# The second token group's plain feature blocks: 8 instead of 10, with block scales built by GpSimd, reordered steps, and one pair of query loads split over two queues

## The chip, the cores and the metric

The kernel runs on one core of a Trainium2 chip. The metric is the device time of one execution in microseconds (us); several executions are made and the median is quoted. One further execution is recorded by the hardware profiler. Engines are named as in the profile: PE is TensorE (PEld its weight loads), DVE is VectorE, ACT is ScalarE, POOL is GpSimd, SP is SyncE, which here only issues transfers; POOL issues transfers too, and "SPq" and "POOLq" are their queues.

## The reference

A retention layer (a linear recurrence with one decay per head) feeds a feed-forward layer whose activation is h * erf(softplus(h)).

```python
# q, k, v: (4, 8, 768, 64) float32
gamma = 1.0 - 2.0 ** (-5.0 - np.arange(H))
for t in range(S):
    state = gamma * state + einsum('bhd,bhe->bhde', k[:, :, t], v[:, :, t])
    y[:, :, t] = (1 / sqrt(D)) * einsum('bhd,bhde->bhe', q[:, :, t], state)
x = y.transpose(0, 2, 1, 3).reshape(B * S, H * D)      # (3072, 512)
h = x @ w_in                                           # w_in (512, 2048), float64
g = h * erf(log1p(exp(h)))
out = g @ w_out                                        # w_out (2048, 512), float64
```

## The kernel before

**Tiling.** The 3072 tokens are 24 chunks of 128 (six per batch), and two chunks make a group of 256: groups 0 to 11. The 2048 hidden features are 16 blocks of 128 (`ft`); a piece of `w_in` holds two blocks (pieces 0 to 7). The order of all work on every engine is written out by hand in the source; each engine runs its own list in that order and waits at an instruction whose inputs or buffer are not ready, with everything behind it on that engine.

**Two ways to make the hidden values.** Plain: `hidden_of` multiplies float32 operands, 256 columns at a time (L698), and needs only the converted weight piece `WF`. Split: weights and x are each cut into hi, lo and dif parts of a faster type, and each product is three matmuls. `unit(g, n)` does that for one group and one piece (two blocks, 256 columns, L732); `pair_unit(g, ft)` does it for one block and two neighbouring groups at once (512 columns, L766). `ALONE` says which blocks a group has by itself: group 0 all 16 plain, group 1 its first 10 plain, the last group half by `unit`. Blocks 10 to 15 of groups 1 and 2 are joined, blocks 8 and 9 of group 2 are done by `unit(2, 4)`, and blocks 0 to 7 of group 2 are joined with group 3 in the period after.

**The first 24 us** do the retention of chunks 0 to 3 (groups 0 and 1) in the simple form (`ret_out`, `ret_add`: copies of x L539, L540, states L547). **The plain loop**, `for ft in range(n_ft)`, then runs over the 16 blocks. Each turn has its matmuls, `need(...)`, which advances the conversion of float64 weights to float32 on DVE (per piece: exponents L235, then L249, L254, L258, L270, with an ACT step L238 between) until the piece wanted next is there, the extra work that the table `during` lists for that `ft`, and `put_hidden`: an ACT copy out of PSUM (L712 for two groups, L709 for one) and a POOL transfer to scratch (L714, L710). The h tiles come from a pool of six (`small`, tag b2). In this loop chunks 4 and 5 (group 2) go through the retention: transposes, `begin` at ft 6, `states` at 7, `results` at 8, `crossed_sums` at 9. Also in the loop: x of groups 1 and 2 is split (`split_x`, L332 on ACT, L333 and L334 on DVE), pieces 4 and 5 are split (`split_weights`: L312 on ACT, L325 and L326 on DVE), and the first block pair of chunks, 6 and 7, is loaded and prepared.

**Pairs of chunks.** `load_pair(j)` loads k and v in rows by POOL (four transfers of 256 KB) and k and q once more in 32-row blocks (`KB`, `QB`) by SP: 16 + 16 transfers of 32 KB (L164), each of 128-byte runs. `prepare(j)` is one DVE transpose of `KB` (L565), a multiplication of `QB` by the table `kq_b` (L560), and a transpose of `QB`. `steps(pair, n)` advances the loads. `load_block_scales` fetches the first column of that table and its factors by 20 small POOL transfers (L407, L413), and `block_scales` finishes it: three DVE instructions (L419 to L421) and five POOL multiplications (L423).

**Periods.** After the loop, period 2 runs `unit(2, 4)` and six joined units, and each later period eight units, with `begin` and `results` of the next pair between them (`joined(at, to, g)`: before unit 3 and unit 5), split weights, the next pair's loads, and each unit's put: for joined units of group 1 two ACT copies and a 512 KB POOL transfer of a high and a low part (L777 to L779, tile in the 34-buffer pool b4), later an ACT and a DVE instruction (L340, L341) into a b2 tile. PSUM banks o0 to o3 alternate between units, so a unit's put must be through before the second unit after it starts. At the end the projection with `w_out` (L981) reads the hidden values back; where they were stored as high and low parts, `add_lows` adds them on DVE (L917).

Of the kernel before, what the change touches and what calls it, by code (L numbers as in the profile page):

```python
# [13 lines left out]
F32 = mybir.dt.float32  # L14
F32R = mybir.dt.float32r
U32 = mybir.dt.uint32
I64 = mybir.dt.int64
AF = mybir.ActivationFunctionType
ALU = mybir.AluOpType
# [13 lines left out]
def head(u, r):  # L33
    return u // 2 + u % 2 * 4 + 2 * r
# [15 lines left out]
def kernel(  # L50
# [23 lines left out]
    DH = d_model // 2  # L74
    FIRST = JPC // 2 - 1

    ALONE = {0: n_ft, 1: 5 * n_ft // 8, NG - 1: n_ft // 2}
    assert D == 64 and d_model == H * D and n_k == HP == 4 and S % GT == 0 and NJ % 2 == 0
    assert H == 8 and n_ft == 16 and NC > JPC and GT == 2 * C

# [69 lines left out]
    def load_pair(j):  # L150

        b, c = divmod(j, NC)
        KNP[j] = b4("kn", [2, H, D])
        KB[j], QB[j] = (b4(name, [HP, 2 * C]) for name in ("kb", "qb"))
        for i in range(2):
            load_values(j + i, nc.gpsimd)
            KN[j + i], SLOT[j + i] = KNP[j][:, i], head
            nc.gpsimd.dma_start(KN[j + i], of_chunk(k, j + i))
        yield
        for to, src in ((KB[j], k), (QB[j], q)):  # L160
            for s, d in itertools.product(range(2), range(2)):
                part = slice((2 * s + d) * 32, (2 * s + d + 1) * 32)
                for u in range(HP):
                    nc.sync.dma_start(  # L164
                        to[part, u].rearrange("p (a d) -> p a d", d=32),
                        src[b, head(u, s), c * C : (c + 2) * C, d * 32 : (d + 1) * 32].rearrange(
                            "(a p) d -> p a d", p=32
                        ),
                    )
                yield  # L170

    kq_s = const.tile([P, NC, 2, H], F32, name="kq_s")
# [226 lines left out]
        query_scale(slice(2, NC))  # L399


    kq_b = const.tile([P, 2, HP, NC, 4], F32, name="kq_b")
    by_b = const.tile([P, 2, HP], F32, name="by_b")

    def load_block_scales():
        for s, i in itertools.product(range(2), range(2)):
            nc.gpsimd.dma_start(  # L407
                by_b[s * D : (s + 1) * D, 1, 2 * i : 2 * i + 2], decay_s[i * D : (i + 1) * D, s::2]
            )
        for s, d in itertools.product(range(2), range(2)):  # L410
            part = slice((2 * s + d) * 32, (2 * s + d + 1) * 32)
            for u in range(HP):
                nc.gpsimd.dma_start(  # L413
                    kq_b[part, 0, u, 0],
                    decay_k[:, head(u, s) : head(u, s) + 1].rearrange("(a p) h -> p (a h)", p=32),
                )

    def block_scales():
        nc.vector.reciprocal(by_b[:, 0], by_b[:, 1])  # L419
        nc.vector.reciprocal(kq_b[:, 1, :, 0], kq_b[:, 0, :, 0])  # L420
        nc.vector.tensor_scalar(kq_b[:, 1, :, 0], kq_b[:, 1, :, 0], unscale, None, op0=ALU.mult)  # L421
        for c in range(1, NC):
            nc.gpsimd.tensor_tensor(  # L423
                kq_b[:, :, :, c], kq_b[:, :, :, c - 1],
                by_b[:, :, :, None].to_broadcast([P, 2, HP, 4]), op=ALU.mult,
            )

    psum_turn = itertools.cycle((ps_r, ps_h))
# [124 lines left out]
    def prepare(j):  # L553


        for name, store, x in (("k", KT, KB[j]), ("q", QT, QB[j])):
            if name == "q":
                own = x.rearrange("p u (a d) -> p u a d", d=32)
                scale = kq_b[:, 1, :, j % NC : j % NC + 2].rearrange("p u c a -> p u (c a)")
                nc.vector.tensor_tensor(  # L560
                    own, own, scale[:, :, :, None].to_broadcast([P, HP, 8, 32]), op=ALU.mult
                )
                yield
            t = b4(name + "T", [HP, 2 * C])
            nc.vector.transpose(t.rearrange("p u t -> p (u t)"), x.rearrange("p u t -> p (u t)"))  # L565
            for i in range(2):
                store[j + i] = t[:, :, i * C : (i + 1) * C]
            yield

        if j > 2 * JPC:  # L570
            yield from values(j)
# [93 lines left out]
    def crossed_sums(j):  # L665
        g, i = divmod(j, 2)
        for r in range(2):
# [4 lines left out]
            else:  # L672
                nc.vector.tensor_tensor(x, x, SC[j][a][:, 2:, :D], op=ALU.add)

    def split_x(j, n=1):
        g, i = divmod(j, 2)
        if i == 0:
            if not XR:
                XR.extend(
                    ring.tile([P, 3, HP, GT], F32R, name=f"x_{x}", tag=f"x{i}")  # L680
                    for i, x in enumerate(("hi", "lo", "dif"))
                )
            X[g] = [x[:, g % 3] for x in XR]
        at = slice(i * C, (i + n) * C)
        split(X[g], (slice(None), slice(None), at), XC[g][:, :, at])

# [151 lines left out]
    ret_out(JPC - 1, lambda: hidden_of(0, 0), state_last=True)  # L838
    need("in", 1)
    hidden_of(1, 0)  # L840
    A(JPC - 1)


    def steps(s, n=1):
# [11 lines left out]
        5: [(scale_early, b, 0), (T, b, None, ("o0", "o1")), (steps, pair, 2)],  # L856
        6: [(begin, a, ps_r), (begin, b, None, ("o2", "o3")), (steps, pair)],
        7: [(states, a), (states, b)],
        8: [(results, a, ("o0", "o1")), (results, b), (block_scales,)],
        9: [(crossed_sums, a), (crossed_sums, b), (convert, 2), (split_x, a, 2)],  # L860
        10: [(hi_of, 4), (steps, vals, 1)],
        12: [(split_weights, 4), (hi_of, 5)],
        13: [(split_x, 2, 2), (steps, vals, 1)],
        14: [(split_weights, 5)],
        15: [(steps, prep, 3)],
    }
# [149 lines left out]
    def period(g, prep, next_prep):  # L1016

        a, b = 2 * g + 2, 2 * g + 3
        one, two = partial(partial, unit), partial(partial, pair_unit)
        if g == G2:  # L1020
            units = [one(g, 4)] + [two(1, ft) for ft in range(ALONE[1], n_ft)]
            return units, joined(3, 5, g), {
                0: [(hi_of, 6)],
                1: [(split_weights, 6)],
                2: [(hi_of, 7)],
                3: [(states, a), (states, b), (split_weights, 7)],
                4: [(hi_of, 0), (split_weights, 0)],
                5: [(crossed_sums, a), (crossed_sums, b), (split_x, a, 2)],
                6: [(hi_of, 1), (split_weights, 1), (steps, next_prep, 1)],
            }, range(4)  # L1030
        if g < NG:
            units = [two(g - 1, ft) for ft in range(8 - 8 * (g % 2), 16 - 8 * (g % 2))]
        if g == G2 + 1:
            return units, joined(3, 5, g), {
                0: [(steps, vals), (hi_of, 2), (steps, prep, 1)],
                1: [(steps, prep, 1), (steps, vals)],
                2: [(split_weights, 2), (hi_of, 3)],
                3: [(states, a), (states, b), (split_weights, 3)],
                5: [(crossed_sums, a), (crossed_sums, b), (split_x, a, 2)],
                7: [(steps, next_prep, 1)],  # L1040
            }, range(4)
        if g < NG - 2:
            return units, joined(2, 5, g), {
                0: [(steps, prep, 4)],
                1: [(convert, 2)],
                2: [(states, a), (convert, 1)],
                3: [(states, b), (convert, 1)],
                4: [(convert, 2 if g < 8 else 1)],
                5: [(crossed_sums, a), (crossed_sums, b)],
                6: [(split_x, a, 2)],  # L1050
                7: [(steps, next_prep, 1 if g < NG - 3 else 4), (convert, 1)],
            }, LOADS.get(g, ())
        if g == NG - 2:
            return units, joined(1, 3, g), {
                0: [(steps, prep, 4), (load_w_out, 0)],
                1: [(states, a), (load_w_out, 1)],
                2: [(states, b), (split_w_out, 0)],
                3: [(crossed_sums, a), (crossed_sums, b)],
                4: [(split_w_out, 1), (load_hiddens, 0)],
                5: [(split_x, a, 2)],  # L1060
                6: [(softplus, 0), (load_w_out, 2)],
                7: [(erf, 0), (gated, 0)],
            }, ()
        if g == NG - 1:
            return units, {}, {
                0: [(split_g, 0), (split_w_out, 2), (load_w_out, 3)],
                1: [(split_g, 1), (load_hiddens, 1)],
                2: [(split_w_out, 3)],
                3: [(softplus, 1), (load_w_out, 4)],
                4: [(erf, 1)],  # L1070
                5: [(split_w_out, 4), (load_w_out, 5)],
                6: [(gated, 1)],
                7: [(split_g, 2), (load_hiddens, 2)],
            }, ()
        return [one(NG - 1, n) for n in range(NPC // 2, NPC)], {}, {
            0: [(split_w_out, 5), (load_w_out, 6)],
            1: [(split_g, 3), (load_w_out, 7)],
            2: [(split_w_out, 6)],
        }, ()
# [92 lines left out]
```

## Time and profile before

| | before |
|---|---|
| median of 3 runs | 608.81 us (608.66 to 609.01) |
| the profiled execution's own time | 608.73 us |
| its span, first to last instruction | 607.0 us |
| DVE busy in the span | 462.4 us (76%) |
| ACT busy | 394.6 us (65%) |
| POOL busy | 131.4 us (22%) |
| mean granted TensorE clock | 1.000 |

The span is what the profile's rows add up to; 1.7 us of the execution lie outside it. In rows of a timeline the columns are start, duration, engine, line, operation, output and input tiles with shapes, and count; in brackets stands how long the engine had been idle just before, and what ended that. In the chain of waits in order of time the columns are start, length and the work. All rows are in us.

### The profile page before, as it was taken

To read this page: it belongs to the slowest core of one execution; us is meant where nothing else is said; L and a number is where in the kernel's file an instruction comes from. 1 tells how busy PE (TensorE), PEld (TensorE's weight loads), DVE (VectorE), ACT (ScalarE), POOL (GpSimd) and SP (SyncE) were. 2 spreads that over 40 slices of the span, in tenths; PEclk is the share of its full clock that TensorE was granted. 3 is DMA by queue.
4 is the path that set the end of the run, shared out by engine and by line. 5 is a ranking of instruction groups with operands and counts; after the bars stand their busy time and mean duration, and the time that the engine had idled before them with its cause. 6 is when DMAs were issued, how large, how long until landed. Compare 5 with 4: busy or idle time off the path is not lost.

```text
span 607.0 us, 13097 instructions
## 1 busy us (share of the span) xinstructions
PE 601.5 (99%) x5160; PEld 501.8 (83%) x5160; DVE 462.4 (76%) x579; ACT 394.6 (65%) x620; POOL 131.4 (22%) x223
## 2 busy tenths in 40 slices
PE   8999999999999999999999999999999999999997
PEld 6888888888888888888888988888888888888886
DVE  5899898877978779787778995887777758668540
ACT  3684858354453544435487787899889888988920
POOL 1086463244535535242111200000000000000000
PEclk9999999999999999999999999999999999999999
DMA  9999698988979999795655937145424432531300
GB/s 202 347 260 263 146 245 259 246 180 233 256 194 277 250 261 209 228 233 169 201 163 183 307 122 240 37 140 173 139 72 137 148 104 96 173 125 49 105 35 35
DMA packets 147692, 109.93 MB, mean 181 GB/s; under 512 B 103152, under 2 KB 127472, under 8 KB 147632
## 3 DMA queue, kind: packets, MB, share of 16 engines
q1 hardware_dynamic: 131536, 59.93, 38.7%
q0 software_dynamic: 15536, 49.04, 25.5%
q8 instruction: 40, 0.66, 0.5%
q14 instruction: 20, 0.16, 0.1%
q10 hardware_dynamic: 560, 0.14, 0.1%
HBM read 71.58 MB, written 37.49 MB: 180 GB/s over the span
## 4 chain that ended last, share of the span: by engine, by line
PE 99%; ACT 0%; POOL 0%; issue 0%; DVE 0%; DVEq 0%; POOLq 0%
PE o L766 34%; PE o L981 22%; PE r L981 11%; PE hp L981 11%; PE hp L698 8%; PE o L732 1%; PE hp L594 1%; PE hp L766 1%; PE r L766 1%; PE hp L643 1%; PE r L643 1%; PE r L594 1%; PE r L654 1%; PE r L601 1%; PE o L526 1%; PE r L487 1%
## 5 line engine op out<-in xcount | busy, mean ns | idle before, releaser
L766 PE MATMUL o<-x_hi,w_hi 128*128 128x512 f32 x296 | 117.3, 396 | 0.0
L766 PE MATMUL o<-x_lo,w_lo 128*128 128x512 f32 x296 | 115.3, 390 | 0.0
L340 ACT ACTIVATE h<-o 128x512 f32<-128x512 f32 x70 | 41.5, 594 | 90.6 <-PE o L766 87.9
L936 DVE TENSOR_TENSOR e<-hid,e 128x1024 f32<-128x1024 f32 x48 | 56.6, 1221 | 53.2 <-ACT e L926 53.2
L766 PE MATMUL o<-x_dif,w_dif 128*128 128x512 f32 x296 | 79.1, 389 | 0.0
L341 DVE SCALAR_TENSOR_TENSOR h<-o,h 128x512 f32<-128x512 f32 x70 | 47.8, 686 | 30.0 <-ACT h L340 25.6
L783 POOL DMA_DIRECT2D hids<-h x72 | 40.4, 562 | 137.3 <-DVE h L341 136.8
L766 PEld LDWEIGHTS o<-x_hi,w_hi 128*128 128x128 f32 x296 | 55.5, 188 | 12.3
L766 PEld LDWEIGHTS o<-x_dif,w_dif 128*128 128x128 f32 x296 | 55.6, 188 | 11.5
L766 PEld LDWEIGHTS o<-x_lo,w_lo 128*128 128x128 f32 x296 | 55.6, 188 | 11.0
L334 DVE SCALAR_TENSOR_TENSOR g_dif<-g_hi,g_lo 128x1024 fp32r<-128x1024 f32 x48 | 58.8, 1225 | 3.6 <-DVE g_lo L333 0.5
L332 ACT ACTIVATE g_hi<-e 128x1024 fp32r<-128x1024 f32 x48 | 51.0, 1062 | 15.3 <-DVE e L936 12.7
L333 DVE TENSOR_TENSOR g_lo<-e,g_hi 128x1024 fp32r<-128x1024 f32 x48 | 58.6, 1221 | 0.1
L922 ACT ACTIVATE e<-hid 128x1024 f32<-128x1024 f32 x48 | 48.3, 1053 | 0.8 <-DVE hid L917 0.6
L926 ACT ACTIVATE e<-e 128x1024 f32<-128x1024 f32 x48 | 48.2, 1052 | 0.3
L981 PE MATMUL o<-w_hi,g_hi 128*128 128x512 f32 x120 | 46.7, 389 | 0.0
L981 PE MATMUL o<-w_lo,g_lo 128*128 128x512 f32 x120 | 46.7, 389 | 0.0
L981 PE MATMUL o<-w_dif,g_dif 128*128 128x512 f32 x120 | 46.7, 389 | 0.0
L698 PE MATMUL hp<-xT,w 128*128 128x256 f32 x208 | 46.3, 381 | 0.0
L698 PEld LDWEIGHTS hp<-xT,w 128*128 128x128 f32 x208 | 39.0, 190 | 5.3
L578 ACT ACTIVATE v<-v,kq_s 128x64 f32<-128x64 f32 x144 | 35.6, 335 | 0.0
L922 ACT ACT_TABLE_LOAD x24 | 30.8, 1283 | 4.2 <-DVE hid L917 2.9
(211 smaller groups left out, 1249.0 us busy)
## 6 DMA issues: line engine op xcount, KB each, us to landing
hids<-h POOLq DMA_DIRECT2D x72, 256.0 KB, 4.0
hid<-hids SPq DMA_DIRECT2D x36, 512.0 KB, 4.9
raw<-in_moe_w_in_dram SPq DMA_DIRECT2D x32, 256.0 KB, 5.5
raw<-in_moe_w_out_dram POOLq DMA_DIRECT2D x32, 256.0 KB, 6.3
out_dram<-y SPq DMA_DIRECT2D x23, 256.0 KB, 2.1
kb<-in_k_dram SPq DMA_DIRECT2D x144, 32.0 KB, 3.9
v<-in_v_dram POOLq DMA_DIRECT2D x18, 256.0 KB, 6.2
kn<-in_k_dram POOLq DMA_DIRECT2D x18, 256.0 KB, 7.1
```

Of the source, the lines that this page charges most:

```text
L332: nc.scalar.activation(hi, x, AF.Copy, scale=KEEP)
L333: nc.vector.tensor_tensor(lo, x, hi.bitcast(F32), op=ALU.subtract)
L334: nc.vector.scalar_tensor_tensor(dif, hi.bitcast(F32), Z, lo.bitcast(F32), op0=ALU.mult, op1=ALU.subtract)
L340: nc.scalar.activation(to, a, AF.Copy, scale=1 + 1 / Z)
L341: nc.vector.scalar_tensor_tensor(to, b, -1 / Z, to, op0=ALU.mult, op1=ALU.add)
L698: nc.tensor.matmul(HP_[bank][:, col], w[:, kk, ft % 2 * P : (ft % 2 + 1) * P], XC[g][:, kk], start=(kk == 0), stop=(kk == n_k - 1),)
L766: nc.tensor.matmul(to, W[n][i][:, kk * 2 * P + u * P : kk * 2 * P + (u + 1) * P], XR[i][:, at, kk], start=(kk == 0 and i == parts[0]), sto ...
L783: nc.gpsimd.dma_start(HID2[g][:, ft % 8], h)
L922: nc.scalar.activation(E[n], HID_[n], AF.Softplus)
L926: nc.scalar.activation(E[n], E[n], AF.Erf)
L936: nc.vector.tensor_tensor(E[n], HID_.pop(n), E[n], op=ALU.mult)
L981: nc.tensor.matmul(Y[g][t][x // 2], G[n][x][:, f, t * P : (t + 1) * P], W_OUT[ft // 2][x][:, ft % 2 * d_model : (ft % 2 + 1) * d_model], s ...
```

## The change

Six edits are made.

- `ALONE[1]` goes from 10 to 8: group 1's blocks 8 and 9 leave the plain loop. Period 2 has eight joined units (blocks 8 to 15) in place of `unit(2, 4)` and six joined ones; `begin` and `results` stay before units 3 and 5.
- The table `kq_b` keeps only its query half. Its first column is copied by POOL from `kq_s` into `first_b` and moved by 16 small POOL transfers; its factors are POOL copies of `d_s`. The three DVE instructions and four small transfers go, and POOL's five multiplications are half as large.
- Two steps of the weight conversion move ahead of the last `ret_add` of the first stage.
- In the loop, two conversion steps move from ft 9 to ft 8, ahead of `results`.
- The splits of x are taken apart (`hi_x`, `lo_x`, `last_x`) and spread over ft 9, 11 and 12, the dif parts behind the split of piece 4; `hi_of` of pieces 4 and 5 move by one turn.
- Of the first pair's 16 query transfers, 8 move from SP to POOL, at ft 3 and 4, ahead of those turns' puts; the steps of `load_pair(6)` are so seven, not nine. Later pairs stay as they were.

```diff
-    ALONE = {0: n_ft, 1: 5 * n_ft // 8, NG - 1: n_ft // 2}
+    ALONE = {0: n_ft, 1: n_ft // 2, NG - 1: n_ft // 2}
...
+        parts = list(itertools.product(range(2), range(2)))
+        for n, (s, d) in enumerate(parts):
+            blocks(KB[j], k, s, d, nc.sync)
+            if n > 1 and j < 2 * JPC:
+                blocks(QB[j], q, 1, n - 2, nc.gpsimd)
+            yield
+        for n, (s, d) in enumerate(parts):
+            if n < 2 or j >= 2 * JPC:
+                blocks(QB[j], q, s, d, nc.sync)
                 yield
...
     def load_block_scales():
+        for s in range(2):
+            nc.gpsimd.tensor_copy(
+                first_b[:, s].rearrange("p (c i) -> p c i", c=2),
+                kq_s[:, 0, 1].rearrange("p (i s c) -> p s c i", i=2, s=2)[:, s],
+            )
+        for s, d, a in itertools.product(range(2), range(2), range(4)):
             nc.gpsimd.dma_start(
+                kq_b[(2 * s + d) * 32 : (2 * s + d + 1) * 32, :, 0, a],
+                first_b[a * 32 : (a + 1) * 32, s],
+            )
...
     def block_scales():
-        nc.vector.reciprocal(by_b[:, 0], by_b[:, 1])
-        nc.vector.reciprocal(kq_b[:, 1, :, 0], kq_b[:, 0, :, 0])
-        nc.vector.tensor_scalar(kq_b[:, 1, :, 0], kq_b[:, 1, :, 0], unscale, None, op0=ALU.mult)
+        for s in range(2):
+            own = slice(s * D, (s + 1) * D)
+            nc.gpsimd.tensor_copy(
+                by_b[own].rearrange("p (c i) -> p c i", c=2),
+                d_s[own].rearrange("p c (i s) -> p s c i", s=2)[:, s],
+            )
         for c in range(1, NC):
             nc.gpsimd.tensor_tensor(
-                kq_b[:, :, :, c], kq_b[:, :, :, c - 1],
-                by_b[:, :, :, None].to_broadcast([P, 2, HP, 4]), op=ALU.mult,
+                kq_b[:, :, c], kq_b[:, :, c - 1], by_b[:, :, None].to_broadcast([P, HP, 4]), op=ALU.mult
             )
...
+    def hi_x(g):
+        place_x(g)
+        nc.scalar.activation(X[g][0], XC[g], AF.Copy, scale=KEEP)
+
+    def lo_x(g):
+        hi, lo, dif = X[g]
+        nc.vector.tensor_tensor(lo, XC[g], hi.bitcast(F32), op=ALU.subtract)
+
+    def last_x(g):
+        hi, lo, dif = X[g]
+        nc.vector.scalar_tensor_tensor(
+            dif, hi.bitcast(F32), Z, lo.bitcast(F32), op0=ALU.mult, op1=ALU.subtract
+        )
...
     hidden_of(1, 0)
+    next(weight_steps)
+    next(weight_steps)
     A(JPC - 1)
...
-        8: [(results, a, ("o0", "o1")), (results, b), (block_scales,)],
-        9: [(crossed_sums, a), (crossed_sums, b), (convert, 2), (split_x, a, 2)],
-        10: [(hi_of, 4), (steps, vals, 1)],
-        12: [(split_weights, 4), (hi_of, 5)],
-        13: [(split_x, 2, 2), (steps, vals, 1)],
+        8: [(convert, 2), (results, a, ("o0", "o1")), (results, b), (block_scales,)],
+        9: [(convert, 1), (crossed_sums, a), (crossed_sums, b), (hi_x, JPC // 2)],
+        11: [(hi_of, 4), (hi_x, 1)],
+        12: [(lo_x, JPC // 2), (lo_x, 1), (split_weights, 4), (last_x, JPC // 2), (last_x, 1), (steps, vals, 1)],
+        13: [(hi_of, 5), (steps, vals, 1)],
         14: [(split_weights, 5)],
...
-            units = [one(g, 4)] + [two(1, ft) for ft in range(ALONE[1], n_ft)]
+            units = [two(1, ft) for ft in range(ALONE[1], n_ft)]
```

## The prediction

> **What bounds the kernel now.** I read the page's busy times and chain first, then the list of waits of PE, then the chain in order of time, and last the timelines of DVE, SP and POOL around the plain loop and period 2. The page puts PE on the chain for 99% of the span:
>
> ```profile
> PE 601.5 (99%) x5160; PEld 501.8 (83%) x5160; DVE 462.4 (76%) x579; ACT 394.6 (65%) x620; POOL 131.4 (22%) x223
> PE 99%; ACT 0%; POOL 0%; issue 0%; DVE 0%; DVEq 0%; POOLq 0%
> PE o L437 <- POOL ident masks.py:199: 1.5, 1, 1.5
> PE r L487 <- ACT kqT L481: 0.3, 1, 0.3
> ```
>
> The last two lines are all of PE's own waits: 1.8 us, in the first 8 us. From there PE is never seen waiting, so only two things can move the end: the amount of matmul work, and a new wait of PE. The chain in order of time gives the price of each sort of matmul:
>
> ```profile
> 39.28 6.91 PE hp L698 x32
> 52.53 7.11 PE hp L698 x32
> 61.66 14.01 PE hp L698 x64
> 75.67 2.87 PE o L732 x24
> 314.43 5.44 PE o L766 x24
> ```
>
> One plain product of 256 columns is two records (26 blocks times 4 products are 104, and the page counts L698 x208); a record costs 6.91/32 = 0.216 us. `unit(2, 4)` is the row at 75.67, 2.87 us. A joined unit is half of the last row, 2.72 us, or 0.227 us a matmul.
>
> **The matmul work.** Removed: two blocks of group 1, 2 x 4 products x 2 records x 0.216 = 3.46 us, and `unit(2, 4)`, 2.87 us. Added: two joined units, 5.44 us. The sum is 5.44 - 3.46 - 2.87 = -0.89 us. All of it lies on PE, so on the path that sets the end.
>
> **When PE would come to each place** (all times on before's clock). `begin` ends at 52.53. Then block 7 for two groups and block 8 for one, 8 records each, 24 x 0.216 + 0.2 for the change of matmul form (7.11 less 32 x 0.216) = 5.4, to 57.9; `results`, 2.02 as between 59.64 and 61.66, to 59.9; 56 records with the same allowance, 12.3, to 72.2. The first joined unit so starts at 72.2, where before `unit(2, 4)` started at 75.67 and the first joined unit at 78.54. It wants hi and lo of x of groups 1 and 2 and of piece 4 at 72.2, and all dif parts eight matmuls later, at 74.0.
>
> **Is DVE there by then?** This is the question of the change, since DVE is the busiest engine of the loop. Its rows of before:
>
> ```profile
> 24.27 0.69 DVE L270 SCALAR_TENSOR_TENSOR w<-w,power 128x512 f32<-128x512 f32 x1
> 26.17 0.42 DVE L547 TENSOR_TENSOR state<-state,o 128x256 f32<-128x256 f32 x1 [1.21 <-PE o L534]
> 26.50 0.42 DVE L235 TENSOR_SCALAR power<-raw 128x512 uint32<-128x512 uint32 x1
> ...
> 55.31 0.17 DVE L419 RECIPROCAL by_b<-by_b 128x4 f32<-128x4 f32 x1
> ...
> 55.74 0.69 DVE L249 TENSOR_SCALAR w<-raw 128x1024 uint32<-128x1024 uint32 x1
> ```
>
> *The two early steps.* They fill the 1.21 us in which DVE waited for PE. Steps L235, L249, L254, L235 are 1.74 us at their spacings (0.34, 0.45, 0.61, 0.34); started at 24.9 they end at 26.6, the state addition follows, and what came at 28.24 comes at 26.95: 1.29 us earlier. Their input is there: the four transfers of piece 1 were issued from 16.36 to 18.73 with 5.8 us to landing, so by 24.5. The price is on ACT: the two L238 (0.72 each) now stand ahead of the copy L540, which ends at about 27.7 in place of 26.99; the plain product that reads it started at 27.8. I take 0.05 us for PE, between 0 and 0.3. DVE then runs without waits to `states`, where PE's `begin` limits it (first half done at 51.61, DVE back at 52.87 before), so 1.15 us are kept.
>
> *The tables.* L419 to L421 occupy DVE from 55.31 to 55.74: 0.43 us gone. `states` so ends at 54.2.
>
> *The new order from there*, in DVE's spacings of before: conversion of piece 6, 4.7 (58.8); first half of the next, 1.5 (60.3); the crossed sums, which want ACT's copies of the results (PE done at 59.9, copies 60.6), 1.0 (61.3); two halves of conversion, 1.4 and 2.4 (65.1); two lo parts at 1.25 (67.6); piece 4, 2.5 (70.1); two dif parts, 2.5 (72.6). Wanted: lo at 72.2, piece 4 at 72.2, dif at 74.0. It fits with 1.4 us, and still with 0.3 if the early start wins nothing. I cost it at nothing; every us beyond 74.0 costs PE one us. On ACT, `hi_x` waits for the crossed sums (61.4 to 62.4) with the put of block 9 behind it (63.0), for whose PSUM bank PE comes at 65.1; the rest of the row (0.58 for each put) is spaced as before.
>
> *After it* piece 5 (75.1; wanted at 77.6 by the third unit), the transposes of pair 6 (kT 76.3, scaling 77.5, qT 78.7). `begin` comes after three joined units, 72.2 + 8.16 = 80.4, where it came at 84.0 before. So 1.7 us are left.
>
> **The transfers.** SP's rows show that it is the slow queue here, and POOL's row shows what a full queue does:
>
> ```profile
> 61.82 9.64 SPq L164 DMA_DIRECT2D qb<-in_q_dram  x16
> 71.56 8.04 SPq L164 DMA_DIRECT2D kb<-in_k_dram  x16
> 79.72 19.17 SPq L164 DMA_DIRECT2D qb<-in_q_dram  x16
> 98.58 0.31 SPq L164 DMA_DIRECT2D qb<-in_q_dram  x1
> 53.07 0.54 POOL L714 DMA_DIRECT2D hid<-h  x1 [0.77 <-DMA v<-in_v_dram]
> ```
>
> The ninth POOL transfer after a first one waits for that one's landing, so eight are in flight at most. Eight of SP's 16 queries go: 8 x 0.60 = 4.8 us, so SP ends with pair 6 at 66.6, lands by 69.2 (2.6 us, the row's median after 62 us) and starts on pair 8 about 5 us sooner. POOL gains eight issues of 256 runs each. No row shows that form there; the nearest are 0.54 (one 128-run put) and 0.89 (1024 runs, L158). I take 0.6, by the number of runs: 4.8 us, at most 7.1. Against this stand four fewer table transfers (0.6 each, from L413), less two to four copies at 0.25 to 0.4 (L373, L423). Behind these issues in POOL's queue are the puts of blocks 3 to 7. With rounds of eight at up to 8.5 us (a k transfer issued at 49.16 freed its place at 57.61) they are issued up to 5 us later than before, the last by about 66. What waits for them is a b2 tile for a later put (block 13's waits for block 4's, which lands by 70 at worst; ACT does not come to it before 70.5), so PE sees nothing. Pair 6's queries land by 70 against 76.3. If that cover were gone, DVE would stand at L560 and each us past 78 would stop `begin`.
>
> The Trainium skill, "DMA: Bandwidth & Descriptors", section "Issuing engines are not separate DMA queues", speaks against this part: transfers issued by several engines run on the same 16 DMA engines, and a second issuer saves only the issuing time. The slices of the page with a DMA share of nine tenths up to 61 us agree with it for that stretch. By that rule alone the queries would land no sooner, which is the first rival below.
>
> **Smaller terms, cost nothing.** One more pair of ACT copies (0.6 each) and 512 KB put in period 2, on an engine 65% busy. One more high and low part to add, 0.69 us of DVE (L917) at 354; it stands before the split of the fifth block of activations, done at 356.6 and wanted by PE at 364.05. If 7 us of cover were gone there, it would cost its 0.69.
>
> **The sum.** -0.89 + 0.05 = -0.84 us against the profiled execution: span 607.0 to 606.2, its time 608.73 to 607.9. The median shown is 0.08 above that execution, so I say 608.0 for the median.
>
> **Rivals.**
>
> *Pair 8's queries come too late (the far side).* The row at 98.58 is the last of 16; with 3.0 us to landing it is there at 101.6, and:
>
> ```profile
> 101.86 1.18 DVE L560 TENSOR_TENSOR qb<-qb,kq_b 128x1024 f32<-128x1024 f32 x1
> 103.19 0.69 DVE L341 SCALAR_TENSOR_TENSOR h<-o,h 128x512 f32<-128x512 f32 x1
> ```
>
> The put of period 3's first unit (L341) stands behind L560 on DVE and ends at 103.9; PE wants its bank two units after 98.96, at 104.4: a cover of 0.5 us. With the change PE comes at 103.5. If the queries land at 101.6 as before, PE stops for 0.4: -0.5 in all. POOL's burst of v, k, `w_out` and hidden values begins at 73 instead of 77; if it falls on these 16 so that one of their two rounds of eight takes the 12.2 us to landing of the worst stretch in place of the 9.0 of the first, they land at 104.8, PE stops 3.6 us, and the time is 610.7. It becomes slower than before from a landing at 102.1, and by 0.2% from 103.3. For it: little slack before. Against: SP is 5 us ahead, and half the 16 are issued before the burst is dense. Chance 16%.
>
> *DVE is the bound at the first joined unit.* If the early start wins nothing and POOL's new copies hold DVE up by their own 1.0 us, the last dif part ends at 74.75 and PE stops 0.7 us: 608.7, no change. To be slower by 0.2% it would take 76.1. For it: DVE busy 4.9 of each 5 us from 30 to 55. Against: DVE beside POOL's five multiplications at 62.07 takes 0.70 for L254, 0.69 elsewhere. Chance 12%.
>
> *The change doesn't do what it says*: the steps move, PE's saving is eaten by small waits at changes of matmul form, 608.8. Chance 5%.
>
> *More than the sum.* With 0.222 a record (7.11/32) and 2.88 for the unit, the gain is 1.0; with a median that falls 0.2 low, as the runs shown scatter by 0.35, it passes 0.2%. Part of the forecast's own case.
>
> **Chances and range.** About 0.2%, 1.2 us, is what a measurement of this kernel can tell from no change. The forecast's case has 62%, 17 of them below 607.6 by pitch and scatter and 45 within 0.2%. The first rival gives 13% slower and 3% within, the second 3% and 9%, the third 5% within, and 5% stays for a slower stop that I haven't found. So faster 17%, same 62%, slower 21%. The forecast's own range is 607.3 to 608.5; taking in the second rival and the lower half of the first, 607.2 to 610.2.
>
> **What would show it.** Right: L698 x192, no L732 before the last group, a first L766 near 72.2 with no idle of PE ahead of it, L766 x12 after it in 2.7 us, `begin` near 80.4, the last x_dif on DVE near 72.6, SP done with pair 6 near 67, and all of PE 0.9 us earlier from period 3 to the end. Wrong: a wait of PE named for DVE x_dif or w_dif near 74, for ACT or DVE h near 103, or an L560 that waits for a transfer while a put stands behind it.

## The result, and the profile after

| | before | after |
|---|---|---|
| median | 608.73 us (608.59 to 609.01, 4 runs) | 615.46 us (614.69 to 616.84, 4 runs) |
| ratio to before | | 1.0112 (95% interval 1.0096 to 1.0127) |
| the profiled execution's own time | 608.73 us | 614.87 us |
| its span | 607.0 us | 613.2 us |
| mean granted TensorE clock | 1.000 | 0.997 |

608.0 us was predicted, with a range of 607.2 to 610.2: the time is 7.5 us above the one and 5.3 above the other. The page of the changed kernel first, its busy times, the shares of the chain and one of the DMA queues:

```profile
PE 602.2 (98%) x5144; PEld 501.2 (82%) x5144; DVE 462.3 (75%) x577; ACT 395.5 (65%) x621; POOL 138.4 (23%) x228
q8 instruction: 40, 0.66, 0.4%
PE 97%; issue 1%; DMA 0%; DVE 0%; ACT 0%; DVEq 0%
```

There is less matmul work (16 instructions fewer), no other engine has come onto the chain, and yet 1% of it is "issue": PE stood while nothing that the profile follows held it. The list of PE's waits names the places:

```profile
PE o L796 <- issue: 3.7, 1, 3.7
PE r L614 <- issue: 0.9, 1, 0.9
```

The chain in order of time (start, length, work) shows what went as forecast and where it broke:

```profile
52.38 5.38 PE hp L728 x24
59.78 12.28 PE hp L728 x56
72.07 8.18 PE o L796 x36
82.28 5.67 PE o L796 x24
89.76 16.55 PE o L796 x72
106.31 0.62 PE hp L607 x32
...
108.33 0.66 PE o L796 x2
108.99 3.65 issue
112.65 6.72 PE o L796 x22
...
121.41 13.82 PE o L796 x60
...
268.34 0.93 issue
269.54 8.38 PE o L796 x36
```

The rows of before that answer to those at 106.31, 121.41 and 269.54 (`begin` of pair 8, the work behind its `results`, and the work behind a later `begin`):

```profile
107.34 0.62 PE hp L594 x32
...
117.09 13.82 PE o L766 x60
...
263.89 8.39 PE o L766 x36
```

So PE is 1.03 us ahead at 106.31, 4.32 behind at 121.41 and 5.65 behind at 269.54. It stays some 5.7 behind to the last group of matmuls (587.38 against 581.65); the end adds 0.44, which is a matter of its own (the last experiment). The sum is the 6.2 us between the spans.

PE's timeline around the first place (start, duration, operation, tiles, count, and in brackets the idle time):

```profile
108.60 0.39 PE L796 MATMUL o<-x_lo,w_lo 128*128 128x512 f32 x1
112.65 0.59 PE L796 MATMUL o<-x_hi,w_hi 128*128 128x512 f32 x1 [3.65 <-issue]
113.03 0.63 PE L796 MATMUL o<-x_lo,w_lo 128*128 128x512 f32 x1
113.46 0.63 PE L796 MATMUL o<-x_hi,w_hi 128*128 128x512 f32 x1
...
116.69 0.39 PE L796 MATMUL o<-x_lo,w_lo 128*128 128x512 f32 x1
```

Two matmuls after `begin`, PE stops for 3.65 us in the middle of a unit, and the matmul that comes late reads from the same tiles of x and of the weights as the first of the two, so it waits for no new tile. Then matmuls follow each other at 0.43 us, where 0.227 is usual, until 116.0. The table by stretches gives the clock of it (the columns are busy times of PE, PEld, DVE, ACT and POOL, then the granted clock, the DMA share and GB/s):

```profile
105.00:110.00 5.00, 3.99 (x136) 3.19 (x135) 4.93 (x10) 1.03 (x2) 2.15 (x4) 1.00 1.11 227
110.00:115.00 5.00, 2.35 (x6) 1.87 (x6) 3.47 (x6) 0.00 (x0) 0.00 (x0) 0.75 1.00 315
115.00:120.00 5.00, 5.00 (x64) 3.87 (x66) 1.23 (x2) 1.20 (x2) 0.55 (x1) 0.91 0.39 96
```

The gap of 4.05 us between two matmuls, less their usual 0.23, and eight or so further matmuls 0.2 us late are the 5.35 us lost here. The Trainium skill, "TensorE: Matmul & The Clock Gate", Part 1, says that the clock falls to half after an idle window of about 3.4 us and returns after as long a busy one, with matmuls of 512 columns 426.7 ns apart meanwhile. The pitch of 0.43 us agrees, and so do the 3.41 us for which the trace's clock records grant one half; the stop that suffices is shorter here (2.0 us in one run below).

**What PE waited for.** Queue q8, "instruction", moved 40 packets, 16,384 bytes each by the trace's DMA records: 40 blocks of 256 instructions are 10,240, and PE has 10,288 matmuls and weight loads. I count PE's records in the trace from the start, with number 0 for the first: the matmuls, the weight loads and 86 waits and the like of its sequencer, 10,374 in all. The first stop comes at record 2497 and the second at 6593: 4096 apart, 16 times 256. Records that lie a multiple of 256 from these I call block borders. The answers on the DMA queues hold the packet that matters; in the kernel before it ran between 99 and 102 us, in the changed one between 110 and 112 and none from 102 to 110. The lines of before, then of after:

```profile
q8 instruction: 1, 0.02, 2.4%
```

```profile
q8 instruction: 1, 0.02, 3.4%
```

By its record it ran at 100.47 before and at 110.20 after, and PE went on 2.45 us behind the latter. From record 449 on there are 40 borders, as many as packets; paired in order, no packet in any trace of this case runs more than 300 records ahead of its border, and the late one of the changed kernel runs when PE already stands at record 2497. So a theory: PE's instructions come in blocks of 256, fetched by the same DMA engines that move the data; a fetch asked for when those queues are full comes late, and `begin` (128 matmuls of 64 columns and their weight loads, 256 instructions in 2.0 us) eats a whole block before it is there.

### The profile page after: what moved, and what is told of

The parts are those of the page before. It is cut to its first block, busy times and chain, and to the rows that moved or that the text cites. A ratio compares the mean times of both kernels' runs of the same rounds, so it can differ in the third digit from the quotient of the medians.

```text
span 613.2 us, 13063 instructions
## 1 busy us (share of the span) xinstructions
PE 602.2 (98%) x5144; PEld 501.2 (82%) x5144; DVE 462.3 (75%) x577; ACT 395.5 (65%) x621; POOL 138.4 (23%) x228
## 4 chain that ended last, share of the span: by engine, by line
PE 97%; issue 1%; DMA 0%; DVE 0%; ACT 0%; DVEq 0%
PE o L796 35%; PE o L1013 21%; PE r L1013 11%; PE hp L1013 11%; PE hp L728 7%; PE o L762 1%; PE hp L607 1%; PE hp L796 1%; PE r L796 1%; PE r L656 1%; PE hp L656 1%; PE r L614 1%; PE r L607 1%; PE r L667 1%; PE r L500 1%
## 5 line engine op out<-in xcount | busy, mean ns | idle before, releaser
L796 PE MATMUL o<-x_hi,w_hi 128*128 128x512 f32 x304 | 121.4, 399 | 3.7 <-issue 3.7
L796 PE MATMUL o<-x_lo,w_lo 128*128 128x512 f32 x304 | 119.2, 392 | 0.0
L796 PE MATMUL o<-x_dif,w_dif 128*128 128x512 f32 x304 | 81.6, 390 | 0.0
L796 PEld LDWEIGHTS o<-x_lo,w_lo 128*128 128x128 f32 x304 | 57.5, 189 | 15.3 <-issue 3.9
L796 PEld LDWEIGHTS o<-x_hi,w_hi 128*128 128x128 f32 x304 | 57.3, 189 | 12.8
L796 PEld LDWEIGHTS o<-x_dif,w_dif 128*128 128x128 f32 x304 | 57.5, 189 | 12.1
L728 PE MATMUL hp<-xT,w 128*128 128x256 f32 x192 | 42.9, 381 | 0.0
L728 PEld LDWEIGHTS hp<-xT,w 128*128 128x128 f32 x192 | 35.9, 190 | 5.0
```

Of the source, the lines that this page charges most:

```text
L728: nc.tensor.matmul(HP_[bank][:, col], w[:, kk, ft % 2 * P : (ft % 2 + 1) * P], XC[g][:, kk], start=(kk == 0), stop=(kk == n_k - 1),)
L796: nc.tensor.matmul(to, W[n][i][:, kk * 2 * P + u * P : kk * 2 * P + (u + 1) * P], XR[i][:, at, kk], start=(kk == 0 and i == parts[0]), sto ...
```

## The experiments

Two theories stand against each other. **Blocks** (B): the one above, so the number of PE's instructions ahead of `begin`, and the time at which POOL's burst of loads starts, decide. **Queues** (Q): one of the other edits, the tables, the reordered steps or the queries on POOL, holds something up near 109. What separates them is a count: the change takes out 16 + 24 matmuls and puts 24 in, so 16 matmuls and 16 weight loads fewer (5144 against 5160 on the page), all ahead of `begin` of pair 8.

**32 and 16 instructions given back, at the very start.** The changed kernel's first idle product is cut into ten pieces (e1) or six (e2):

```diff
-    keep_warm(7)
+    for i in range(10):
+        at, to = 7 * P * i // 10, 7 * P * (i + 1) // 10
+        nc.tensor.matmul(idle.rearrange("p a b -> p (a b)")[:, : to - at], ident, ident[:, : to - at], ...
```

> The changed kernel with PE's first idle matmuls cut into ten pieces instead of two, so that 32 more PE instructions stand ahead of everything else, as many as the removed plain products had; no other edit. Theory B (instruction blocks): PE stopped at 109 us because the 16 KB block of its next 256 instructions was fetched behind data transfers; with the count of before the border of the blocks stands 32 instructions earlier against begin(8), so its fetch starts about 3.6 us sooner (32 at 0.113 us), ahead of the burst: no stop near 109, and the predicted sum comes true, 607.6 to 608.5 us. Theory Q (queues): the moved transfers or tables delay something that PE needs, whatever its count: 613 to 617 us, stop at 109 as before.

Measured 609.63 us (609.03 to 610.91; ratio 1.0016, 1.0007 to 1.0026). The stop and the later one are gone; the fetch ran at 100.56. The time is 1.1 us above the range. The trace shows two reasons: the pieces themselves take 4.57 us where the idle product took 3.35, and there is a stop of 0.3 us at 59.0, at record 1217 (5 x 256 short of 2497).

> The same with six pieces, 16 more PE instructions. Theory B: the fetch starts 1.8 us sooner, the stop at 109 shrinks but need not go: 608 to 613 us. Theory Q: 613 to 617 us.

Measured 613.51 us, which no single execution had: of ten, five lie from 609.5 to 610.8, four from 616.3 to 617.1 and one at 620.3 (ratio 1.0069, 1.0033 to 1.0105). The median is 0.5 us above the range of B and inside that of Q, so it separates nothing; the two clusters do, for with half of the instructions back the same program goes either way. In the profiled execution, one of the upper five, the stop is there; none of the lower five was profiled.

**The split of the blocks alone, and everything but it.** The kernel before with `ALONE[1]` at 8 and eight joined units (e3); the changed kernel with that one edit undone (e4):

```diff
-    ALONE = {0: n_ft, 1: 5 * n_ft // 8, NG - 1: n_ft // 2}
+    ALONE = {0: n_ft, 1: n_ft // 2, NG - 1: n_ft // 2}
-            units = [one(g, 4)] + [two(1, ft) for ft in range(ALONE[1], n_ft)]
+            units = [two(1, ft) for ft in range(ALONE[1], n_ft)]
```

> The kernel before with one part of the change alone: 8 plain blocks for group 1 and eight joined units in period 2. Tables, steps and queues are those of before. PE's count is that of the changed kernel. Theory B: a stop of 1 to 6 us in period 3 near begin(8) or at the border after it: 609.5 to 615 us. Theory Q: the sum of the matmul work alone, 607.8 to 608.3 us, as the queues and tables are not touched.

> The changed kernel with the first part undone: ten plain blocks for group 1, unit(2, 4) and six joined units in period 2; tables, steps and queues as changed. PE's count is that of before. Theory B: no stop near begin(8), 608.3 to 609.2 us. Theory Q: the stop stays, 613 to 617 us.

Measured: e3 615.96 us (612.78 to 618.86; ratio 1.0118, 1.0081 to 1.0156), e4 608.83 us (608.45 to 609.0; ratio 1.0002, 0.9992 to 1.0011). e3 is 1 us above the range of B and e4 is inside it. The loss comes with the split of the blocks alone, without the tables, steps or queues, and without the split it is absent: theory Q falls. e3's waits of PE also show, in the last line, what the other edits are for:

```profile
PE o L766 <- issue: 3.1, 1, 3.1
PE r L601 <- issue: 1.5, 1, 1.5
PE o L654 <- issue: 0.6, 1, 0.6
PE o L766 <- DVE x_lo L333: 0.3, 1, 0.3
```

Without the early and reordered steps and the shorter tables, the second matmul of the first joined unit waits 0.3 us for the split of x, until 73.40.

**32 instructions in another place.** The changed kernel with 16 of period 2's 512-column matmuls, in blocks 14 and 15, made two of 256 columns each:

```diff
+            if g == 1 and (ft == 15 or ft == 14 and parts == (2,)):
+                for kk, i, t in itertools.product(range(n_k), parts, range(2)):
+                    nc.tensor.matmul(to[:, t], W[n][i][...], XR[i][:, (at.start, at.stop - 1)[t], kk], ...
```

> The changed kernel with three dif-and-hi stretches of period 2 (the third part of block 14, all of block 15, both ahead of the begin of pair 8) cut from 512-column matmuls into twice as many 256-column ones: 16 matmuls more, 32 PE instructions more, nothing else moved. By the rows the cut costs about 0.15 to 0.3 us of PE (unit(2, 4), in 256 columns, took 2.87 us where a joined unit takes 2.72). Theory blocks (PE stops because its next block of 256 instructions is fetched after the burst of transfers begins): the borders of the blocks stand to begin as in the kernel before, the fetch runs near 100.5 us, no stop at 109, and the time is 608.0 to 608.6. Theory queues (the tables, the reordered steps or the queries on POOL hold something up at 109): nothing changes, 613 to 617.

Measured 608.85 us (608.32 to 609.59; ratio 1.0, 0.9991 to 1.0009), 0.25 us above the range: no stop at 109, fetch at 100.42. As in e1, there are small stops, at records 1217 and 1985, two more block borders, where the next matmul starts 0.3 us late each time; with the longer end that the last experiment treats they are part of what keeps it from 608.

**The same taken from the kernel before.** 16 matmuls of the third part left out in period 2:

```diff
+            last = n_k
+            if g == 1 and parts == (2,):
+                last = 1 if ft < 15 else 3
-            for kk, i in itertools.product(range(n_k), parts):
+            for kk, i in itertools.product(range(last), parts):
```

> The kernel before with 16 matmuls of the third (dif) part left out in its joined units of period 2 (blocks 10 to 14 keep one of four, block 15 three of four; a small correction of these hidden values is missing): 32 PE instructions fewer ahead of the begin of pair 8, and 16 x 0.227 = 3.6 us less matmul work. Queues, tables and steps are those of before. Theory blocks: the fetch that ran at 100.5 us is now asked for when the burst of v, k, w_out and hidden values is already under way, or close to it, and PE stops near begin for 1 to 6 us: 606 to 611, with a stop named issue of 1 us or more near 105 to 110. Theory queues: no stop of PE's own, 608.7 - 3.6 = 605.1.

Measured 613.35 us (613.02 to 614.41; ratio 1.0076, 1.0063 to 1.0088). The kernel before with 3.6 us less work takes 4.5 us longer: 2.4 us above even the range of B, since three borders stop it:

```profile
PE o L769 <- issue: 3.7, 1, 3.7
PE r L601 <- issue: 1.2, 1, 1.2
PE hp L654 <- issue: 1.1, 1, 1.1
```

None of the change's other edits is in this kernel.

**What delays the fetch.** The changed kernel with period 3's w_out loads moved to its last four units (e7); with the same move and POOL's row loads (v and kn, 1 MB) of pair 10 behind `begin` (e10); with the same move and the row loads of all pairs from 10 on behind it (e9). The expectation of e10 says that the w_out loads stay; its edit moves them too, as the second line of this diff, which all three share, shows:

```diff
-            }, range(4)
+            }, range(4, 8)
...
-            load_values(j + i, nc.gpsimd)
-            nc.gpsimd.dma_start(KN[j + i], of_chunk(k, j + i))
+        ROWS.append(rows)
...
             put()
+            if i == 3 and ROWS:
+                ROWS.pop()()
```

> The changed kernel with period 3's four w_out loads (256 KB each, from POOL) moved from its first four units to its last four: 1 MB less in the DMA queues between 99.7 and 110 us, PE's instructions unchanged. Theory blocks, with the delay of the fetch made by the transfers that share its DMA engines: the fetch that took until 110.2 lands sooner, the stop at 109 shrinks by 1 us or more, and the time is 609 to 613.5. If the fetch is late for another reason than these transfers: 614 to 617, stop as it was.

> The changed kernel with POOL's four row loads (v and kn, 1 MB) of each pair from pair 10 on issued after the fourth unit of its period instead of the first, so behind begin, and with period 3's four w_out loads moved to its last four units. PE's instructions and their order are those of the changed kernel. Theory blocks: the fetch asked for near 103 us, and the one asked for near 262, meet only SP's small transfers; both run within about 2 us, there is no stop at 109 nor at 268, and the time is 607.9 to 609.0. If the block is late because PE asks for it too late whatever the transfers do: the stop stays, 612 or more.

> The same for pair 10 alone (period 3), the w_out loads left where the changed kernel has them. Theory blocks: the stop at 109 goes or is under 1 us if v and kn delayed the fetch, the later one at 268 stays (0.9 to 1.2 us): 609 to 611. If w_out's loads and the puts are enough to delay it: 612 to 615.

Measured: e7 614.1 us (613.33 to 615.58; ratio 1.0092, 1.0078 to 1.0106), 0.6 us above the range of B and just inside the other one, whose condition, the stop as it was, does not hold: the packet came at 109.15, 1.05 us earlier, and the stop fell from 3.65 to 2.5 us. e10 610.24 us (608.41 to 610.79; ratio 1.002, 1.0011 to 1.0029): the stop at 109 is gone with PE's instructions unchanged, the one at 263 stays, 1.5 us. e9 608.85 us (608.4 to 609.18; ratio 1.0002, 0.9993 to 1.0011): both are gone. So the burst delays the fetch. Moving w_out away takes 1.05 us off, and moving the v and kn rows of pair 10 away as well (e7 against e10) takes off the rest of the stop; the rows alone, with w_out left in place, were not run. The packet still took 2.5 us from the request in e9 and e10, beside SP's transfers, a little more than expected.

**The burst brought forward in the kernel before**, four row loads of pair 10 issued in period 2's last unit:

```diff
+            if g == G2 and i == len(units) - 1:
+                ahead.append(load_pair(2 * g + 6))
+                next(ahead[0])
```

> The kernel before, its instructions of PE unchanged, with POOL's four row loads of pair 10 (1 MB) issued in the last unit of period 2, ahead of that unit's put, at about 98 us instead of 102.05. Theory blocks: the fetch that ran at 100.5 us is now asked for in the burst and runs several us later; PE needs it at 109.4 to 111.6, so it stops 0 to 3 us: 609 to 613, and in the trace the fetch is later than 102 either way. Theory that the number of PE's instructions alone makes the stop: nothing changes, fetch at 100.5, 608.5 to 609.

Measured 608.85 us (608.71 to 609.01; ratio 1.0002, 0.9993 to 1.001), and the fetch ran at 99.96, at once: a miss of B as I had put it. The rows were first issued at 98.97, later than planned, and the next table says why that was not enough.

**All of it in one table.** In the runs in which the fetch ran at once, it ran while PE was at records 2205 to 2208; so I take the start of record 2206 for the time at which it was asked for. "Rows" is POOL's first v load of period 3, "lead" how long it was out when the fetch was asked for. The last two columns are the starts of record 2496, the last before the border, and of record 2497. All us.

| kernel | rows | asked | lead | packet ran | PE at 2496 | at 2497 |
|---|---|---|---|---|---|---|
| e9 | 115.48 | 103.49 | -11.99 | 105.94 | 109.12 | 109.35 |
| e12 | 115.32 | 103.33 | -11.99 | 106.39 | 108.96 | 109.19 |
| e10 | 115.16 | 103.17 | -11.99 | 105.73 | 108.80 | 109.03 |
| before | 102.05 | 100.38 | -1.67 | 100.47 | 108.96 | 108.96 |
| e1 | 100.75 | 100.40 | -0.35 | 100.56 | 108.97 | 108.97 |
| e5 | 100.95 | 100.62 | -0.33 | 100.42 | 109.20 | 109.20 |
| e4 | 100.71 | 100.44 | -0.27 | 100.41 | 109.02 | 109.02 |
| e11 | 98.97 | 99.92 | 0.95 | 99.96 | 108.75 | 108.79 |
| e2 | 100.12 | 101.58 | 1.46 | 110.22 | 108.51 | 112.69 |
| e6 | 99.78 | 101.73 | 1.95 | 109.11 | 107.59 | 111.68 |
| e3 | 102.37 | 104.35 | 1.98 | 110.71 | 109.98 | 113.44 |
| after | 99.70 | 102.97 | 3.27 | 110.20 | 108.60 | 112.65 |
| e7 | 99.82 | 103.09 | 3.27 | 109.15 | 108.72 | 111.65 |
| e8 | 100.35 | 103.62 | 3.27 | 112.34 | 113.00 | 114.74 |

A fetch asked for from 1.67 us ahead of the first row load to 0.95 us behind it runs at once; from 1.46 us behind on it waits 6 to 9 us, and e2, at the edge, went both ways. With the rows moved behind `begin` (e9, e12 with e9's edits, e10) it waits 2.5 to 3.1 us and is still in time. Where PE stopped, it goes on 2.4 to 2.7 us behind the start of the packet. The edge, between 0.95 and 1.46 us, was read off after these runs; no run was made to test it.

**The queries on one queue.** The changed kernel with the first pair's queries all on SP:

```diff
-            if n > 1 and j < 2 * JPC:
-                blocks(QB[j], q, 1, n - 2, nc.gpsimd)
...
-            if n < 2 or j >= 2 * JPC:
-                blocks(QB[j], q, s, d, nc.sync)
-                yield
+            blocks(QB[j], q, s, d, nc.sync)
+            yield
```

> The changed kernel with the first pair's queries all on SP again, as before; PE's instructions as in the changed kernel. Theory blocks: the stop at 109 stays, 612 to 617. Theory queues: without the queries on POOL, POOL's burst starts later (the v transfers of period 2 near 77 again) and there is no stop: 609 or less.

Measured 615.45 us (612.48 to 616.3; ratio 1.0102, 1.0083 to 1.0122): no better, as B has it (the v load of period 3 moved by 0.65 us only). But the loss is made up otherwise, and PE's stop at the border is only 1.3 us. PE's waits, DVE's timeline, and the chain's rows of `begin`:

```profile
PE o L793 <- DVE h L349: 2.0, 1, 2.0
PE o L793 <- issue: 1.3, 1, 1.3
PE r L611 <- issue: 0.9, 1, 0.9
```

```profile
106.13 1.23 DVE L570 TENSOR_TENSOR qb<-qb,kq_b 128x1024 f32<-128x1024 f32 x1 [7.35 <-DMA kb<-in_k_dram]
107.27 0.68 DVE L349 SCALAR_TENSOR_TENSOR h<-o,h 128x512 f32<-128x512 f32 x1
```

```profile
109.40 1.06 PE hp L604 x32
110.47 0.85 PE hp L611 x32
111.32 0.85 PE r L604 x32
112.17 0.56 PE r L611 x32
```

This is the mechanism of the prediction's first rival: pair 8's queries late, the multiplication of `QB` at 106.13, the put of period 3's first unit behind it, PE stopped for 2.0 us. The row names a transfer of k for the wait, but the multiplication doesn't read k: SP was done issuing the queries at 101.72, the last of them landed at 105.76, and the k transfer issued right behind it landed at 105.96. What the rival did not count is the clock: behind the 2.0 us it was granted by half (0.50 from 109 to 112 us), and `begin` took 3.3 us where it took 2.0. In the changed kernel pair 8's last query landed at 95.94 (100.94 before), that multiplication stands at 98.11, and PE doesn't wait.

**The last 0.43 us.** In e9 the last group of matmuls starts 0.28 us earlier than before (581.37 against 581.65), and the span is 0.1 longer. The first line of each answer on the chain gives the span, the last piece the end of DVE's work (SP's closing instructions follow); before, then e9:

```profile
core 0 of [0], span 607.0 us
...
603.94 0.33 DVEq L1168
```

```profile
core 0 of [0], span 607.1 us
...
603.66 0.33 DVEq L1214
```

That is 3.06 us against 3.44. The trace's SP records show why. SP closes by waiting in a fixed order for eight counters (100 to 108, without 104) that its and ACT's transfers use in turn. The change takes eight transfers from these engines (the queries, a full turn) and adds one, the read of the additional low part, so the last store moved from counter 108, the last in the order, to 100, the first, and seven waits of 0.062 us each come behind it. One transfer fewer, in e9's kernel, should turn the rotation back:

```diff
-        for g in range(0, n_k, each):
+        for g, each in ((0, 1), (1, 1), (2, 2)) if n == 6 and each == 1 else [(g, each) for g in range(0, n_k, each)]:
```

> The kernel of e9_late_rows with the four transfers of w_in's piece 6 (256 KB each, SP, near 40 us) made three, so one transfer fewer on the engines that issue to the hardware queue. In e9_late_rows the last matmuls begin 0.28 us earlier than in the kernel before, and the span is 0.1 us longer: behind the last addition (DVE L1127 of the kernel before) there come 3.44 us in place of 3.06. SP's closing waits go through eight counters in a fixed order, and the last transfer of the result uses the first of them (100) where it used the last (108) in the kernel before; behind the one that lands last SP still has seven waits, 0.062 us each, 0.43 us. Theory counters: one transfer fewer turns the rotation back, the last transfer uses the last counter, the tail is 3.0 to 3.1 us and the time 608.3 to 608.6. If the longer tail has another cause: 608.85 again, tail 3.4. The stops stay away in both cases.

```profile
core 0 of [0], span 607.2 us
...
604.12 0.33 DVEq L1214
```

The closing part is 3.08 us again, as the theory of the counters says; DVE's last addition ends 2.72 to 2.73 us before the end in the five profiled executions with counter 108 and 3.15 to 3.17 in the nine with counter 100. The median is 608.63 us (608.09 to 609.42; ratio 0.9998, 0.9989 to 1.0007), the lowest median here and still no measurable difference to before. Its profiled execution, at 608.95, has small stops of 0.2 and 0.4 us at records 1217 and 6593; "the stops stay away" so failed in part.

## Why the prediction was wrong

The step that failed is the second paragraph's: "From there PE is never seen waiting, so only two things can move the end: the amount of matmul work, and a new wait of PE." The new wait was then looked for in data alone: tiles that other engines or transfers deliver. PE's own instructions are a transfer too. They stood on the page (40 packets in queue q8) and in the change (fewer matmuls), and no term or named rival counted them; only the 5% for "a slower stop that I haven't found" leaves room for one. What the runs showed in its place: the packet for record 2497, asked for at 102.97 by the table, ran 7.2 us later, PE stood for 3.65 us and then ran at half the clock, 5.35 us in all; a later border cost 1.3 and the end 0.44. The 62% for the forecast's own case rested on a list of resources that was one short.

- *The matmul work*: right. The first joined unit starts at 72.07 (72.2 forecast) with no wait, `begin` of pair 6 at 80.25 (80.4), and at `begin` of pair 8 PE is 1.03 us ahead (0.84 to 1.0 forecast). Of these, 0.17 stood at 21.94 already (22.11 before), ahead of all changed work of PE, so some 0.86 is the change's.
- *DVE's order*: right. The last dif part of x ends at 71.70 (72.6 forecast), and e3, without the early steps, the shorter tables and the new order, shows PE waiting for the split.
- *The transfers*: right in what PE sees. SP ends with pair 6 at 65.78 (66.6 forecast). POOL's row loads began at 73.90 in period 2 (73 forecast) and 2.35 us earlier than before in period 3; I asked only what that does to the queries. With `begin` reached earlier and 32 instructions fewer ahead of it, the request moved from 1.67 us before the first row load to 3.27 behind it.
- *The first rival* named the right neighbourhood, POOL's burst near 100 us, and a real mechanism (e8), but not the one that came; DVE waited for no query here. Its far end is also added up wrong: 608.8 with a stop of 3.6 us and the gain of 0.89 is 611.5, not 610.7.
- *Smaller terms, cost nothing*: one of them, the additional pair of high and low parts, brings the one transfer more and with it 0.43 us of closing waits, nothing on DVE.
- *The gain*: with the stops removed (e9) the 0.89 us is still not in the median. Of 1.03 at most, 0.5 is left at the end of `begin` of pair 8 and 0.28 at the last matmuls. At record 1985 a matmul starts 0.33 us late; the rest goes in steps too small to place. The closing waits take what is left.

What stays open: where between queue and engine the packet waits 6 to 9 us, which no record shows. The small stops at records 1217 and 1985 fit the same account: in the fourteen traces PE stops there where it reaches the border so soon that it goes on only 2.33 to 2.68 us behind the start of the packet (nine times), and it passes these two borders without a stop, or with one under 0.1 us, where the packet started 2.70 us or more before. Why the packet is the earlier in some executions stays open too.

## What to carry to other kernels

Where PE is busy all the time, its instructions are a stream with a deadline: find the instruction packets in the DMA records, and look where a run of very short matmuls (256 instructions in 2.0 us here) meets a burst of loads. A kernel can stand some 3 us from a 5 us loss without a wait in its profile (before, the fetch was asked for 1.67 us ahead of the rows, and the edge lies 0.95 to 1.46 behind them), and an edit that changes the count of PE's instructions, or the start of the burst, can cross that line. Issuing the burst behind the short matmuls removed the long stops here (e9), at no measurable cost against the kernel before, and without a measurable gain.

## What the runs showed that I had not expected

- The Trainium skill, "Runtime: NRT & Kernel Launch", section "Instruction fetch mechanics", says that an engine's instructions are refilled by a DMA queue of its sequencer, in 16 KiB blocks of 256, and that crossing a block border is mostly hidden. The sizes agree: 16,384 bytes, stops a multiple of 256 records apart. The hiding does not hold here: up to 4.0 us of idle at one border, and over 1 us in seven of the fourteen kernels profiled.
- After the first 7 us, PE's idle stops of 2.0 us (e8) and more were followed by half the granted clock, for 3.41 us each time (6.83 in e2's profiled execution); those of 1.5 us (e10) and less were not.
- POOL's five table multiplications, with half the elements, took 5.79 us where they took 2.01, beside a DVE that was then at work without a break; the cause was not tested. In e8 they took 3.12. Nothing waited for them:

```profile
65.98 5.79 POOL L437 TENSOR_TENSOR kq_b<-kq_b,by_b 128x16 f32<-128x16 f32 x5
```
